# A two-layer decode kernel (cached attention and a gated feed-forward): one load of keys per layer cut by columns, its last columns brought in by five transfers of unequal height

## The chip, the cores and the metric

The kernel runs on one core of a Trainium2 chip. The metric is the device time of one execution in microseconds (us); lower is better. An engine here is one of the core's compute engines (TensorE = PE, VectorE = DVE, ScalarE = ACT, GpSimd = POOL) or the queue SP, which issues every transfer of this kernel. "DMA engine" means one of the sixteen movers that carry the transfers' rows.

## The reference, cut to what matters

Two layers, each an attention block over a cache followed by a feed-forward block, for 4 sequences of one token:

```python
def _A_ref(x, k_cache, v_cache, wq, wo):           # 32 query heads, 8 key heads, Dh = 128
    q = (x @ wq) as (4, 32, 1, 128)
    scores = einsum("bhqd,bhkd->bhqk", q, k) * Dh ** -0.5     # 8192 cached keys
    o = einsum("bhqk,bhkd->bhqd", softmax(scores), v)
    return o as (4, 1, 4096) @ wo
def _B_ref(x, w_gate, w_up, w_down):
    return (silu(x @ w_gate) * (x @ w_up)) @ w_down
...
for two layers:
    x = x + _A_ref(_layernorm(x), A_k_cache, A_v_cache, A_wq, A_wo)
    x = x + _B_ref(_layernorm(x), B_w_gate, B_w_up, B_w_down)
```

Both layers read the same caches and weights. Keys and values are 67 MB each in bf16 and are read almost wholly in each layer, so the work is mostly reading: 272.90 MB by the page.

## The kernel before, in words

**Units and slots.** The work of a layer is 16 units: a unit u is one sequence and one pair of key heads (`pair_gb`). Each unit has a load of keys, K(L, u), and one of values, V(L, u), of 4 MB each: 128 partitions with a row of 32 KB (16384 bf16 numbers) per partition, contiguous in memory. A load goes to one of four slots (five in layer 1) of the tile `kvf`; a slot is eight column blocks of 4 KB per partition (`NB = 8`, `BW` numbers wide), named `s{slot}.{q}`.

**What is done with a load.** For keys, `turn` (line 482) transposes each of the eight blocks on DVE in place, then `scores` (line 506) runs four matmuls on the block on PE; `max_p`, `exps` and `turn_p` make the probabilities. For values, `products` (line 608) runs the matmuls; DVE then gathers them (`gather`, lines 660 and 663).

**What sets the order of the loads.** The list `cmds`, written out before any instruction is emitted: K of unit 0, then K and V in turn, V one unit behind; the output weights `wo` in four parts in between; at a layer's end the weights of the feed-forward ("W", "W+"). An entry is (item, slot, first block, end block). `placed` gives slots in turn; some loads are given in halves or in smaller parts there. `pump` issues the next entries of the list as soon as all blocks of an entry are free; `freed` calls it whenever blocks are done with. All go through the queue of SP, in order: `load` calls `T.dma` (line 93), which puts the waits on SP, issues one transfer and counts its semaphore up by 16 on completion. A load of all eight blocks uses the slot's own semaphore (`sem_s`), a partial one a semaphore of its own (`part_sem`).

**Around the change.** `order[0][4]` is the fifth unit of layer 0, `order[1][5]` the sixth of layer 1. The fifth K of layer 0 goes to slot 3, after the third K, and is followed on SP by a V and by the last part of `wo`; the sixth K of layer 1 goes to slot 2, and is followed by a V.

**How the pieces are released.** Slot 3 held keys, which `finished` frees block by block as PE is through with each; slot 2 held values, which are freed by halves of four blocks.

Of the kernel before, what the change touches and what calls it, by code (L numbers as in the profile page):

```python
# [20 lines left out]
class _Sync:  # L21
# [69 lines left out]
    def dma(self, engname, out_ap, in_ap, sem, reads=(), writes=()):  # L91
        self._wait(engname, self._need(reads, writes))
        ins = self.eng[engname].dma_start(out_ap, in_ap)  # L93
        k = id(sem)
        self.semval[k] = self.semval.get(k, 0) + 16
        ins.then_inc(sem, 16)
        self._record(engname, (sem, self.semval[k]), reads, writes)
        return ins

    def wait_res(self, engname, reads=(), writes=()):  # L100
        self._wait(engname, self._need(reads, writes))


def bass_interleave_layers__gqa_block_cached__swiglu_ffn__decode_kernel(
# [18 lines left out]
    P = 128  # L123
# [6 lines left out]
    NB = 8  # L130
# [14 lines left out]
    with ExitStack() as es:  # L145
# [3 lines left out]
        BW = TB * Dh  # L149
# [6 lines left out]
        kv = kvf[:, 0:(NSLOT + 1) * SL].rearrange("p (s w) -> p s w", s=NSLOT + 1)  # L156
# [104 lines left out]
        sem = lambda name: es.enter_context(nc.semaphore(name))  # L261
# [9 lines left out]
        def part_sem():  # L271
# [4 lines left out]
        T = _Sync(engines, prog)  # L276
# [6 lines left out]
             reads=["ident"], writes=["ident"])  # L283
        T.op("pool", lambda e: e.memset(quad[:], 0.0), writes=["quad"])
        for a in range(NA):
# [10 lines left out]
             reads=["ident"], writes=["head"])  # L296
# [3 lines left out]
             reads=["ident"], writes=["made"])  # L300
        T.op("dve", lambda e: e.tensor_reduce(sel[:].rearrange("p (h r) -> p h r", h=2),
                                              made.rearrange("p (h q r) -> p h r q", h=2, q=QH), AX.X, ALU.max),
             reads=["made"], writes=["sel"])
        T.op("dve", lambda e: e.tensor_reduce(own[:], made.rearrange("p (h q r) -> p q h r", h=2, q=QH),
                                              AX.XY, ALU.max),
             reads=["made"], writes=["own"])
# [7 lines left out]
        def pair_gb(u):  # L314
            return u // B, u % B

        order = [list(range(NP)), [NP - 1, NP - 2, NP - 3] + list(range(NP - 3))]
        turn_of = {}

        K = lambda L, u: ("K", L, u)  # L320
# [13 lines left out]
        def placed(seq, ring, parts):  # L334
            out = []
            for i, it in enumerate(seq):
                s = ring[i % len(ring)]
                out += parts[i](it, s) if i in parts else [(it, s, 0, NB)]
            return out
# [4 lines left out]
        cmds = placed(seq, (0, 1, 2, 3), {len(seq) - 1: ends})  # L344
# [7 lines left out]
        s = W_SLOT[0]  # L352
# [5 lines left out]
        assert W_SLOT[1] == ring[len(seq) % len(ring)]  # L358
        cmds += [(("W", 1), W_SLOT[1], 0, NB), (("W+", 1), W_SLOT[1], NB, NB + 1)]

        free = {(s, q) for s in range(NSLOT) for q in range(NB)}
        slot_of = {}
        issued = [0]
# [36 lines left out]
        def pump():  # L400
            while issued[0] < len(cmds):
                it, s, a, b = cmds[issued[0]]
                if it[0] == "wo":
                    load_weight(*it)
                else:
                    need = {(s, q) for q in range(a, b)}
                    if not need <= free:
                        return
                    free.difference_update(need)
                    if it[0] in ("W", "W+"):  # L410
                        load_weight(it[0], it[1], s)
                    else:
                        slot_of[it] = s
                        load(it, a, b, sem_s[s] if b - a == NB else part_sem())
                issued[0] += 1
# [3 lines left out]
        def load(it, a, b, sm):  # L419
            kind, L, u = it  # L420
            s = slot_of[it]
            gp, bt = pair_gb(u)
            src = (A_k_cache if kind == "K" else A_v_cache)[bt, 2 * gp:2 * gp + 2, :, :].rearrange(
                "h (p t) d -> (h p) (t d)", t=TT)
            over = WQ if s == QS and not q_gone else []
            q_gone.update(over)
            T.dma("sp", kv[:, s, a * BW:b * BW], src[:, a * BW:b * BW], sm,
                  writes=[f"s{s}.{q}" for q in range(a, b)] + over)

        def freed(s, a, b):  # L430
            free.update((s, q) for q in range(a, b))
# [403 lines left out]
        for kt in range(KT):  # L835
            T.op("pe", lambda e: e.matmul(xb[:, kt * B:(kt + 1) * B], lhsT=xio[:, pick2(kt)],
                                          rhs=ident[0:B, 0:B], is_transpose=True, start=True, stop=True),
                 reads=["pb", "ident"], writes=[f"pb{OUTB}"], sig=(kt == KT - 1))
# [62 lines left out]
```

## Time and profile before

| | |
|---|---|
| median of 2 runs | 649.96 us (649.75 to 650.18) |
| the profiled execution | 649.47 us |
| its span, first to last instruction | 647.7 us |
| busy, share of the span | PE 66%, DVE 65%, ACT 6%, POOL 2% |
| bytes read by transfers | 272.90 MB |
| chain that ended last, by engine | DMA 61%, DVE 24%, PE 9% |
| SP issuing one load of keys | 327 ns at the least, 328 in the median |

The median is of unprofiled runs, so a sum that is made on the profiled execution (649.47) stands 0.49 below it. The span leaves out 1.8 us of the execution. In the views, "SPq" is SP's queue as it issues a transfer, "kvf<-in_A_k_cache_dram" is a load of keys into the slots, and "us to landing" runs from a transfer's issue to its sixteenth semaphore count. The queue "hardware_dynamic" carries the kernel's own transfers; "instruction" are packets that bring the engines' own instructions, on the same DMA engines.

### The profile page before, as it was taken

What the parts mean: (1) busy time and instruction counts of PE and PEld (TensorE: products, weight loads), DVE (VectorE), ACT (ScalarE), POOL (GpSimd) and SP (SyncE); (2) the same over time, 40 slices, a digit from 0 to 9 for tenths busy, and PEclk for the clock granted to TensorE, in tenths of its full rate; (3) what the DMA queues carried; (4) which work ended last, traced back from release to release, by engine and by line L of the source; (5) the groups of instructions that cost most, each with busy time, mean ns of one, the idle gap of its engine ahead of it and who ended that gap; (6) DMA issues with size and microseconds to landing.
All of it is one profiled execution on the core that took longest, in us unless ns stands there. A gap on an engine that the chain in (4) does not pass through costs nothing.

```text
span 647.7 us, 7963 instructions
## 1 busy us (share of the span) xinstructions
PE 429.5 (66%) x3356; PEld 185.2 (29%) x3356; DVE 422.7 (65%) x703; ACT 39.1 (6%) x109; POOL 11.1 (2%) x43
## 2 busy tenths in 40 slices
PE   2584467466776665767866988767656567666866
PEld 2221122122222222323236333223222222222235
DVE  1585467466776666777852878968766667766943
ACT  1000000000000000000010010000000000000010
POOL 0000000000000000000000000000000000000000
PEclk9996796688977789876975799997778898777976
DMA  9999999999999999999999999999999999999996
GB/s 365 442 423 419 445 426 423 424 439 430 425 435 435 422 438 433 422 442 424 426 413 405 402 433 436 431 428 435 430 431 431 428 431 434 429 428 436 428 413 246
DMA packets 14771, 273.41 MB, mean 422 GB/s; under 512 B 1416, under 2 KB 1424, under 8 KB 5648
## 3 DMA queue, kind: packets, MB, share of 16 engines
q1 hardware_dynamic: 14736, 272.91, 98.9%
q8 instruction: 26, 0.43, 0.3%
q14 instruction: 9, 0.07, 0.0%
HBM read 272.90 MB, written 0.00 MB: 421 GB/s over the span
## 4 chain that ended last, share of the span: by engine, by line
DMA 61%; DVE 24%; PE 9%; issue 3%; another core or an unknown queue 1%; SPq 1%; ACT 0%; DVEq 0%; ACTq 0%
DMA kvf<-in_A_k_cache_dram 51%; DVE kvf L482 18%; DMA kvf<-in_A_v_cache_dram 7%; PE ps L506 4%; DMA kvf<-in_B_w_down_dram 4%; DVE pT L547 2%; PE ps L608 2%; DVE pb L663 2%; SPq L93 1%; PE ps L742 1%; DVE pb L660 0%; DVE kvf L447 0%; PE ps L517 0%; PE ps L697 0%
## 5 line engine op out<-in xcount | busy, mean ns | idle before, releaser
L506 PE MATMUL ps<-kvf,zq 128*128 128x512 bf16 x1024 | 300.3, 434 | 166.9 <-DVE kvf L482 162.5
L482 DVE STREAM_TRANSPOSE kvf<-kvf 128x1024 f32<-128x1024 f32 x246 | 290.2, 1216 | 135.1 <-DMA kvf<-in_A_k_cache_dram 134.8
L506 PEld LDWEIGHTS ps<-kvf,zq 128*128 128x128 bf16 x1024 | 94.7, 108 | 322.1 <-DVE kvf L482 224.5
L608 PE MATMUL ps<-kvf,pT 128*32 128x512 bf16 x960 | 67.1, 402 | 9.2 <-DVE pT L547 9.2
L533 ACT ACTIVATE pb<-ps,tiny 128x512 bf16<-128x512 f32 x32 | 22.0, 687 | 549.9 <-DVE tiny L531 369.7
L547 DVE STREAM_TRANSPOSE pT<-pb 64x512 bf16<-64x512 bf16 x60 | 40.9, 682 | 1.0
L663 DVE SCALAR_TENSOR_TENSOR pb<-ps,tiny,pb 128x128 f32<-128x128 f32 x96 | 33.7, 351 | 5.4 <-PE ps L608 2.1
L608 PEld LDWEIGHTS ps<-kvf,pT 128*32 128x32 bf16 x960 | 21.9, 98 | 37.6 <-issue 22.6
L512 DVE TENSOR_REDUCE tiny<-ps 128x1 f32<-128x512 f32 x32 | 21.9, 685 | 5.1 <-PE ps L506 4.5
L668 PEld LDWEIGHTS ps<-sel,pb 128*128 128x128 f32 x64 | 16.7, 274 | 18.0 <-DVE pb L663 10.1
L520 DVE TENSOR_REDUCE m<-ps 1x8 f32<-1x128 f32 x32 | 8.8, 275 | 17.9 <-PE ps L517 17.9
L496 POOL TENSOR_TENSOR zq<-scr,tiny 128x64 bf16<-128x64 bf16 x30 | 9.0, 299 | 562.4 <-PE ps L506 562.4
L668 PE MATMUL ps<-sel,pb 128*128 128x8 f32 x64 | 12.9, 274 | 6.2 <-DVE pb L663 6.2
L551 PE MATMUL ps<-rsm,tiny 128*128 128x8 f32 x64 | 12.0, 261 | 6.3 <-ACT rsm L535 6.3
L551 PEld LDWEIGHTS ps<-rsm,tiny 128*128 128x128 f32 x64 | 10.6, 198 | 18.8 <-ACT rsm L535 16.2
L528 PEld LDWEIGHTS ps<-m,tiny 1*128 1x128 f32 x64 | 10.0, 194 | 15.9 <-issue 13.3
L528 PE MATMUL ps<-m,tiny 1*128 1x8 f32 x64 | 12.9, 272 | 0.8 <-DVE rl L554 0.3
L660 DVE TENSOR_SCALAR pb<-ps,tiny 128x128 f32<-128x128 f32 x32 | 10.1, 316 | 3.4 <-PE ps L608 3.4
L554 DVE RECIPROCAL rl<-ps 128x8 f32<-128x8 f32 x32 | 5.6, 176 | 7.8 <-PE ps L551 7.8
L697 PE MATMUL ps<-oT,wo_sb 128*128 128x4 bf16 x256 | 7.7, 165 | 4.1 <-DVE oT L688 4.1
L742 PE MATMUL ps<-xn,kvf 128*128 128x4 bf16 x256 | 7.6, 166 | 3.6 <-DMA kvf<-in_A_wq_dram 2.8
L535 ACT ACTIVATE rsm<-head,tiny 128x8 f32<-128x8 f32 x32 | 9.6, 300 | 1.0
(73 smaller groups left out, 119.2 us busy)
## 6 DMA issues: line engine op xcount, KB each, us to landing
kvf<-in_A_k_cache_dram SPq DMA_DIRECT2D x28, 4096.0 KB, 32.0
kvf<-in_A_v_cache_dram SPq DMA_DIRECT2D x27, 4096.0 KB, 36.4
kvf<-in_A_v_cache_dram SPq DMA_DIRECT2D x4, 2048.0 KB, 19.0
kvf<-in_A_k_cache_dram SPq DMA_DIRECT2D x4, 2048.0 KB, 9.5
kvf<-in_A_wq_dram SPq DMA_DIRECT2D x2, 2048.0 KB, 9.7
wo_sb<-in_A_wo_dram SPq DMA_DIRECT2D x4, 1024.0 KB, 41.7
kvf<-in_A_v_cache_dram SPq DMA_DIRECT2D x4, 1024.0 KB, 34.8
kvf<-in_B_w_gate_dram SPq DMA_DIRECT2D x2, 1792.0 KB, 25.4
```

The costliest lines, as they stand in the source:

```text
L482: T.op("dve", lambda e: e.transpose(w, w), reads=[f"s{s}.{q}"], writes=[f"s{s}.{q}"])
L506: T.op("pe", lambda e: e.matmul(bank(bk)[:, 0:SW], lhsT=zq[:, z0:z0 + P], rhs=w[:, :, c // 2, :, c % 2], start=(q == 0 and c == 0), stop=( ...
L512: T.op("dve", lambda e: e.tensor_reduce(mx[:], bank(bk)[:, 0:SW], AX.X, ALU.max), reads=[f"pb{bk}"], writes=["mx"])
L528: T.op("pe", lambda e: e.matmul(at, lhsT=onesf[0:1, :].to_broadcast([1, P]), rhs=m8[:, turn_of[u], :], start=True, stop=True), reads=[f"m8 ...
L533: T.op("act", lambda e: e.activation(pb[:], bank(bk)[:, 0:SW], ACTF.Exp, bias=nm, accum_out=rs), reads=[f"pb{bk}", "nm"], writes=PB + ["rs"])
L547: T.op("dve", lambda e: e.transpose(dst, pb[hp]), reads=["pb"], writes=[name])
L551: T.op("pe", lambda e: e.matmul(at, lhsT=ones, rhs=rsm[:], start=True, stop=True), reads=["rsm", "onesf"], writes=[name])
L608: T.op("pe", lambda e: e.matmul(bank(k)[j * QB:(j + 1) * QB, q0 * Dh:q1 * Dh], lhsT=p_t[:, t, h, :], rhs=v[:, q0:q1, t, :], start=(h == 0 ...
L660: T.op("dve", lambda e: e.tensor_scalar(acc, o, own[:, 0:1], None, op0=ALU.mult), reads=[f"pb{k}", "own"], writes=PB)
L663: T.op("dve", lambda e: e.scalar_tensor_tensor(acc, o, own[:, q:q + 1], acc, op0=ALU.mult, op1=ALU.add), reads=[f"pb{k}", "own", "pb"], wr ...
L668: T.op("pe", lambda e: e.matmul(at, lhsT=acc, rhs=sel[:], start=True, stop=True), reads=["pb", "sel"], writes=[name])
L742: T.op("pe", lambda e: e.matmul(at[:, h * B:(h + 1) * B], lhsT=wq_sb[:, kt, h * Dh:(h + 1) * Dh], rhs=xn[:, kt * B:(kt + 1) * B], start=(k ...
```

## The change

In `cmds`, the entry of K(0, order[0][4]) and that of K(1, order[1][5]) are replaced by two: blocks 0 to 6 (28 KB of each row), and block 7 (the last 4 KB of each row). The second entry is not one transfer of 128 partitions but five, of 112, 8, 4, 2 and 2 partitions, in this order, with one semaphore that counts to 80. Both entries get a semaphore of their own instead of the slot's. Every other load is issued as before, by a function that now takes a list of cuts, with one cut from 0 to 128.

```diff
+    def dma_rows(self, engname, out_ap, in_ap, sem, cuts, reads=(), writes=()):
+        self._wait(engname, self._need(reads, writes))
+        k = id(sem)
+        for a, b in zip(cuts[:-1], cuts[1:]):
+            self.eng[engname].dma_start(out_ap[a:b], in_ap[a:b]).then_inc(sem, 16)
+            self.semval[k] = self.semval.get(k, 0) + 16
+        self._record(engname, (sem, self.semval[k]), reads, writes)
...
+        uneven = set()
+        for it in (K(0, order[0][4]), K(1, order[1][5])):
+            i, c = next((i, c) for i, c in enumerate(cmds) if c[0] == it)
+            cmds[i:i + 1] = [(it, c[1], 0, NB - 1), (it, c[1], NB - 1, NB)]
+            uneven.add((it, 1))
...
-            T.dma("sp", kv[:, s, a * BW:b * BW], src[:, a * BW:b * BW], sm,
-                  writes=[f"s{s}.{q}" for q in range(a, b)] + over)
+            T.dma_rows("sp", kv[:, s, a * BW:b * BW], src[:, a * BW:b * BW], sm,
+                       (0, 112, 120, 124, 126, P) if (it, b - a) in uneven else (0, P),
+                       writes=[f"s{s}.{q}" for q in range(a, b)] + over)
```

On SP this is what the two places become, in the built program's order (numbers per partition, two bytes each):

```
layer 0                                         layer 1
K 128x14336   waits for PE and DVE              K 128x14336   waits for PE
K 112x2048    waits for PE and DVE              K 112x2048
K   8x2048                                      K   8x2048
K   4x2048                                      K   4x2048
K   2x2048  twice                               K   2x2048  twice
V 128x16384   waits for PE                      V 128x16384   waits for PE and DVE
```

PE, ACT and POOL keep their instructions in their order. On DVE the first and the eighth transpose of the two K wait for the two new semaphores, where the first waited for the slot's.

## The prediction

> **What bounds the kernel now.** I read the page from the transfers inwards, since parts 2 and 3 answer at once whether the DMA engines ever rest. First the busy share of the sixteen DMA engines over 40 slices, their rate, and the queues:
>
> ```profile
> DMA  9999999999999999999999999999999999999996
> GB/s 365 442 423 419 445 426 423 424 439 430 425 435 435 422 438 433 422 442 424 426 413 405 402 433 436 431 428 435 430 431 431 428 431 434 429 428 436 428 413 246
> ...
> q1 hardware_dynamic: 14736, 272.91, 98.9%
> q8 instruction: 26, 0.43, 0.3%
> q14 instruction: 9, 0.07, 0.0%
> ```
>
> The stream never stops before the last slice, and 98.9% of the sixteen engines' time is the kernel's own packets. The rate is flat near 430 GB/s but for the start, the layer boundary (slices 21 to 23, 402 to 413) and the end. PE and DVE at 66% and 65% have a third of their time left. The chain of waits names the places where the stream sets the time:
>
> ```profile
> 68.09 31.96 DMA kvf<-in_A_k_cache_dram
> ...
> 326.74 23.68 DMA kvf<-in_B_w_down_dram
> 350.47 1.06 PE ps L818 x32
> ...
> 589.43 44.74 DMA kvf<-in_A_v_cache_dram
> 634.22 0.62 PE ps L608 x16
> ```
>
> The columns are start, length, what. A load of keys issued at 68.09 lands 31.96 later, though a load takes about 9.7 alone (below): some 22 us of other transfers stand ahead of it. The last two links are the ones that bind: the feed-forward of layer 0 starts when its last weights have landed (350.42), and the tail of the kernel when the last piece of values has (634.17). Behind that stands 13.5 us of serial work to 647.7. So only what brings those two landings forward or back counts.
>
> SP's queue shows the two places of the change, layer 0 and layer 1:
>
> ```profile
> 68.09 0.33 SPq L93 DMA_DIRECT2D kvf<-in_A_k_cache_dram  x1
> 70.70 0.33 SPq L93 DMA_DIRECT2D kvf<-in_A_v_cache_dram  x1
> 71.08 0.43 SPq L93 DMA_DIRECT2D wo_sb<-in_A_wo_dram  x1
> ...
> 391.74 0.33 SPq L93 DMA_DIRECT2D kvf<-in_A_k_cache_dram  x1
> 402.99 0.33 SPq L93 DMA_DIRECT2D kvf<-in_A_v_cache_dram  x1
> ```
>
> After the K, SP has 2.61 us free in layer 0 and 11.25 in layer 1.
>
> Last, not on the page, the trace's semaphore counts and packets one by one. Every transfer on 128 partitions adds sixteen, one per DMA engine. The first load of keys counts from 22.26 to 24.38, a spread of 2.1 us; the last piece of values from 629.55 to 634.18, a spread of 4.6. So the DMA engines do not keep step, and the landing is that of the slowest. Followed packet by packet (an engine's next packet starts within 20 ns of the last one's end), what sets an engine back is the "instruction" queues: each 16 KB packet of q8 costs its engine some 1.55 us, its own 1.0 to 1.1 and a slowed neighbour, and each 8 KB packet of q14 0.7 to 1.0. In layer 0 the q8 packets go round eight engines in turn. The four engines that carried the four rows of x at the start (four packets of 1 KB, one on each) are never among them; they and four others get only q14, one of the four three times. At the end eight engines stand 2.3 to 4.7 us behind the first, and the worst of the rest 3.9.
>
> **The change part by part.** *Prices of rows*, from landings. The V issued at 70.70 landed 39.1 later, at 109.80; the K before it at 68.09 + 32.0 = 100.09; so a load of eight 32 KB rows per engine is 9.71, 1.214 a row. A `wo` part issued at 35.09 landed 33.3 later, at 68.39, behind a V that landed at 34.72 + 31.1 = 65.82: 2.57 for sixteen 4 KB rows per engine, 0.161 a row. On a line through both, a row costs 0.011 and 0.0376 per KB, so a 28 KB row is 1.064.
>
> *Splitting by columns.* Each engine's eight rows become eight of 28 KB and, evenly dealt, eight of 4 KB: 8.51 + 1.29 = 9.80 against 9.71, 0.09 more per layer for each engine. All of it is on the stream.
>
> *Uneven dealing.* Of the 4 KB rows, the x rows show that a narrow transfer puts one row on each of as many engines, always engines outside the q8 round. I take it that 112 partitions give seven rows to each of sixteen engines, 8 give one to each of the eight engines outside the round, and 4, 2 and 2 fall to the first of these. Then the round's eight get 7 rows, four get 8, two get 9, two get 11. Per layer: the round's eight 8.51 + 7 x 0.161 = 9.64, that is 0.07 less than 9.71; the next four 0.09 more; two 0.25 more; two 8.51 + 1.77 = 10.28, 0.57 more. A transfer's closing semaphore packet is 9 ns; one to five more per engine are under 0.05 and within the rounding.
>
> *What of it reaches the end.* In layer 0 the last landing is that of one of the round's eight (two stand some 3.2 back at the last weights), so 350.42 comes 0.07 earlier and with it layer 1's loads, which wait for PE there. In layer 1 the worst of the round's eight again carries the landing at 634.17: 0.07 more. Sum -0.14, from 0 if the row price is a little higher to -0.30 if the second cut costs nothing (4 KB at 0.152 taken away twice). Above, if the two engines with 11 rows were the last ones, 2 x 0.57 = +1.14. I take -0.14: the eight hold the last place in both layers.
>
> *SP.* The K's issue of 0.33 becomes six of 0.33, 1.98, and one wait more. In layer 0 the first piece may go when block 6 is through, before 68.09, and five remain: 1.65 of the 2.61 before the V's own wait ends. In layer 1 all six fit in 11.25. Queued behind are V and `wo`, then K; nobody is late. Without that cover the V would be issued 1.65 later, into a backlog of 22 us, and cost nothing still; from that backlog on it would cost one for one.
>
> *Waits on DVE.* The first transpose now waits for 28 KB rows alone and may start 1.2 earlier; the eighth waits for the five pieces. Between them stand seven transposes of 1.14 to 1.2 each (8 us), so a landing 0.57 later is hidden. If it were not, PE's scores and the slot's release would be late by at most that, again into the backlog. An earlier start is worth nothing either, as the next load is already queued.
>
> [...]
>
> **The rivals.** *The overloaded two end last.* One engine outside the round has three q14 packets in layer 1 and stands 0.8 short of the last. With 11 rows twice it gains 0.57 + 0.07 on the round's eight in each layer and may pass them in layer 0, where it is within 0.7 of the last. For: nothing shows which of the four engines it is. Against: two of four are loaded so. Price: at most +1.14, as above, so up to 651.1; with one layer +0.3.
>
> *The 112 rows are not spread over sixteen engines.* Slower: no row of this trace has a height that is not a multiple of 16, but for x with 4. On n engines each takes 112 / n rows of 0.161, against seven. On one engine 18.0, 16.9 more than its seven, per layer: since every later load needs that engine too, both reach the end, 650 + 34 = 684. On two, 9.0, 7.9 more: 666. On four, 3.4 more: 657. It decides (2%, 13 us) from two engines down. The x rows on four engines speak against it.
>
> [...]
>
> *A transfer's fixed time stays in the queue.* The nearest row of a transfer alone is the store of the output, 4 KB: 0.29 to issue and 1.0 that SP waits for it, 1.3. If each of the ten more held the stream for that, +13: 663. Against it stands the `wo` part, with at most 0.14: ten times that is 651.4. [...]
>
> *The split frees the slot's waiters earlier and this shows.* Faster: 1.2 us earlier on DVE, twice, 647.6; from slots to landing there are 22 us of backlog, so no.
>
> That the change is not made at all is out: SP's program has the ten pieces.
>
> **How the numbers follow.** Forecast, the round's eight carry the end: 0.72. The overloaded two: 0.20. Rows of 112 on few engines, 0.03, fixed times 0.01. Earlier release 0.01. Something that no row shows, 0.03. The profiled execution has 649.47 - 0.14 = 649.33; the median of the runs shown stands 0.49 above it, and I give the time in its terms: 649.96 - 0.14 = 649.8. The range goes from 649.8 less the spread of the runs (0.7) and the other 0.16 of the gain, 648.9, to 650.18 plus 1.14, 651.3. Two per cent is 13 us, about what a measurement of this kernel can tell from no change: only the 112 rows on one or two engines, the fixed times and half of the unknown pass it. Faster 0.01, within 0.95, slower 0.04.
>
> **What would show it.** In the changed kernel's trace: four or five narrow issues of 0.33 on SP behind the K at 68 and at 392; the V behind at 70.7 and 403 as before; the landing of the last piece of values 0 to 0.3 earlier, its sixteen counts closer together; packets of 4 KB 256 more. Wrong would be: a gap in the stream near 100 or 419, one engine tens of rows behind, a spread at the end over 4.6, or a last landing later than 634.2.

## The result, and the profile after

The changed kernel takes 654.47 us (median of 2 runs, 654.02 to 654.92) against 649.96: a ratio of 1.0074, 95% interval 1.0058 to 1.0091. That is within the 2% and yet clearly slower, by 4.5 us; the prediction had 649.8, and its range ended at 651.3. The profiled span went from 647.7 to 653.1.

The page of the changed kernel, DMA share, rate and queues:

```profile
DMA  9999999999999999999999999999999999999996
GB/s 376 428 423 420 438 406 391 422 435 426 439 425 431 434 422 442 423 437 424 433 407 404 392 436 434 377 426 431 432 425 429 434 429 434 427 434 432 430 410 234
...
q1 hardware_dynamic: 15056, 272.91, 98.8%
q8 instruction: 26, 0.43, 0.3%
q14 instruction: 9, 0.07, 0.0%
```

The bytes are the same and the engines look as busy as before, in every slice. But the rate has two dents that were not there: 406 and 391 in the sixth and seventh slice (82 to 114 us; 426 and 423 before), and 377 in the 26th (408 to 425; 431 before). These are the two places of the change. "Busy" here is the time that a packet took, however slowly it went.

SP's queue in the changed kernel, at the two places (L104 is the `dma_start` in the new `dma_rows`):

```profile
66.96 2.81 SPq L104 DMA_DIRECT2D kvf<-in_A_k_cache_dram  x6
70.75 0.35 SPq L104 DMA_DIRECT2D kvf<-in_A_v_cache_dram  x1
...
394.30 2.10 SPq L104 DMA_DIRECT2D kvf<-in_A_k_cache_dram  x6
405.55 0.35 SPq L104 DMA_DIRECT2D kvf<-in_A_v_cache_dram  x1
```

Nothing is late there: the V is issued at 70.75 (70.70 before), and in layer 1 at 405.55, which is 402.99 plus the 2.56 that layer 0 had lost by then. The chain of waits shows what came of it:

```profile
66.96 33.53 DMA kvf<-in_A_k_cache_dram
...
329.69 23.30 DMA kvf<-in_B_w_down_dram
353.03 1.05 PE ps L833 x32
...
594.54 44.45 DMA kvf<-in_A_v_cache_dram
639.03 1.04 PE ps L623 x16
```

The last weights of layer 0 land at 352.99 instead of 350.42, 2.57 later; the last piece of values at 638.99 instead of 634.17, 4.82 later. Each place costs 2.2 to 2.6 us, and together they hold 4.8 of the 5.4 that the span grew by. The V behind the changed K of layer 0 landed 41.3 after its issue at 70.75, at 112.05, against 109.80: 2.25 of the loss is there within some ten microseconds of the change.

To see it, one cuts out 96 to 102 us, in which the 4 KB rows pass. In these windows the columns are the stretch, its length, busy time of PE, PEld, DVE, ACT and POOL, the granted clock, the DMA share, and GB/s. First the kernel before, then the changed one:

```profile
96.00:102.00 6.00, 0.63 (x2) 0.28 (x3) 1.93 (x2) 0.00 (x0) 0.00 (x0) 0.56 1.00 431
102.00:112.00 10.00, 9.98 (x37) 4.09 (x35) 9.83 (x17) 1.08 (x3) 0.00 (x0) 0.75 1.02 419
```

```profile
96.00:102.00 6.00, 0.19 (x1) 0.13 (x2) 1.49 (x2) 0.00 (x0) 0.00 (x0) 0.50 1.03 274
102.00:112.00 10.00, 9.65 (x37) 3.90 (x36) 9.86 (x17) 1.08 (x3) 0.00 (x0) 0.81 0.95 397
```

The DMA share is 1.03, full, and the rate 274 for 431: 36% of six microseconds is 2.2 us. In the trace's packets of that stretch a 4 KB row takes 284 ns in the median (96.5 to 98 us), not the 160 of the sum, and the 28 and 32 KB rows that other engines are moving at that time take up to 2.17 and 2.13 us instead of 1.07 and 1.22. So the rows of the new transfers are slow, and what is beside them at that time is slow too.

The place in layer 1 shows the same, before and after:

```profile
414.00:424.00 10.00, 7.50 (x56) 2.53 (x54) 8.98 (x15) 0.00 (x0) 0.30 (x1) 1.00 1.04 447
```

```profile
414.00:424.00 10.00, 8.45 (x60) 2.80 (x59) 9.10 (x15) 1.08 (x3) 0.30 (x1) 1.00 1.03 346
```

447 GB/s became 346, and that is 2.3 us of the ten.

### The profile page after: what moved, and what is told of

It reads as the page before. It is cut to its first block, busy times and chain, and to the rows that moved or that the text cites. A ratio compares the mean times of both kernels' runs of the same rounds, so it can differ in the third digit from the quotient of the medians.

```text
span 653.1 us, 7974 instructions
## 1 busy us (share of the span) xinstructions
PE 429.6 (66%) x3356; PEld 185.3 (28%) x3356; DVE 422.6 (65%) x703; ACT 39.1 (6%) x109; POOL 11.1 (2%) x43
## 4 chain that ended last, share of the span: by engine, by line
DMA 61%; DVE 26%; PE 6%; issue 4%; another core or an unknown queue 1%; SPq 1%; ACT 0%; DVEq 0%; ACTq 0%
DMA kvf<-in_A_k_cache_dram 51%; DVE kvf L497 19%; DMA kvf<-in_A_v_cache_dram 7%; DMA kvf<-in_B_w_down_dram 4%; PE ps L623 2%; DVE pT L562 2%; DVE pb L678 2%; PE ps L521 1%; SPq L93 1%; PE ps L757 1%; DVE pb L675 0%; DVE kvf L462 0%; PE ps L532 0%; PE ps L712 0%
## 5 line engine op out<-in xcount | busy, mean ns | idle before, releaser
L543 PEld LDWEIGHTS ps<-m,tiny 1*128 1x128 f32 x64 | 10.1, 197 | 15.2 <-issue 12.8
L675 DVE TENSOR_SCALAR pb<-ps,tiny 128x128 f32<-128x128 f32 x32 | 10.1, 317 | 3.4 <-PE ps L623 3.4
```

The lines of the kernel that those rows point to most:

```text
L543: T.op("pe", lambda e: e.matmul(at, lhsT=onesf[0:1, :].to_broadcast([1, P]), rhs=m8[:, turn_of[u], :], start=True, stop=True), reads=[f"m8 ...
L675: T.op("dve", lambda e: e.tensor_scalar(acc, o, own[:, 0:1], None, op0=ALU.mult), reads=[f"pb{k}", "own"], writes=PB)
```

## The experiments

Three theories went in. *Height*: a transfer that is not 128 high deals the partitions to the DMA engines otherwise, and engines then meet at the same partitions. *Columns*: 4 KB rows 32 KB apart in memory are slow. *Narrow*: transfers of 8, 4, 2 and 2 partitions hold up the engines. Edits are shown against the changed kernel; each time stands beside runs of the kernel before on the same chip.

**e1_cols_only**

```diff
-                       (0, 112, 120, 124, 126, P) if (it, b - a) in uneven else (0, P),
+                       (0, P),
```

> The two K are cut by columns as in the change (28 KB and 4 KB of each row), but the 4 KB come as one transfer of 128 partitions. Three theories for the 2.2 us per layer that the change lost. Height: a transfer of 112 partitions deals the partitions to the sixteen DMA engines otherwise than one of 128, engines meet on the same partitions and slow each other and the loads beside them. Columns: 4 KB rows that stand 32 KB apart in memory are read slowly at any height. Narrow: the transfers of 8, 4, 2 and 2 partitions hold up the engines. Height and narrow say 650.1 here (0.09 per layer for shorter rows), with 4 KB packets of 0.16 us; columns says 654.4, with 4 KB packets near 0.3 us.

Measured 649.59 against 649.10, ratio 1.0004 (0.9995 to 1.0013). The window:

```profile
96.00:102.00 6.00, 1.85 (x5) 0.71 (x6) 3.08 (x5) 0.00 (x0) 0.00 (x0) 0.58 1.02 434
```

434 GB/s: the dent is gone, and the 4 KB rows there take 159 ns in the median and 172 at the most. Columns falls. The split by itself costs nothing that can be told from zero.

**e2_112_16**

```diff
-                       (0, 112, 120, 124, 126, P) if (it, b - a) in uneven else (0, P),
+                       (0, 112, P) if (it, b - a) in uneven else (0, P),
```

> As the change, but block 7 comes as two transfers of 112 and 16 partitions, none narrower than sixteen, so that each DMA engine gets eight rows of 4 KB. Height says the loss stays, 653.5 to 654.5, and 4 KB packets near 0.3 us from the first rows on; narrow says 650.1; columns says 654.4. With even dealing the spread of the landings should not grow in any theory.

Measured 653.50 against 649.10, 1.0068 (1.0055 to 1.0081), nearly all of the loss:

```profile
96.00:102.00 6.00, 0.23 (x1) 0.13 (x2) 1.54 (x2) 0.00 (x0) 0.00 (x0) 0.50 1.01 264
```

Narrow transfers are not needed for it, nor is uneven dealing: here each engine has eight rows, if the 112 are dealt seven to each of sixteen. Narrow falls as the main cause.

**e3_64_64**

```diff
-                       (0, 112, 120, 124, 126, P) if (it, b - a) in uneven else (0, P),
+                       (0, 64, P) if (it, b - a) in uneven else (0, P),
```

> As the change, but block 7 comes as two transfers of 64 partitions, four rows of 4 KB for each engine in each. Height says that engines meet in pairs if each takes four neighbouring partitions, so that a 4 KB row takes up to twice 0.16: 8 x 0.16 = 1.3 us more per layer, 652.6, and less than that if the dealing keeps the engines apart; narrow says 650.1; columns says 654.4.

Measured 654.54 against 649.10, 1.0084 (1.0069 to 1.0099):

```profile
96.00:102.00 6.00, 0.00 (x0) 0.00 (x0) 1.04 (x1) 0.00 (x0) 0.00 (x0) 0.63 1.06 263
```

Two tall, even transfers of 64 rows lose no less than the change. Height had the direction and missed the size: +5.4, where meeting in pairs was to give +2.6.

**e4_narrow_alone**: the K of both layers uncut, and in layer 0

```diff
+                    T.dma_rows("sp", wres[112:, 0:BW], src[112:, (NB - 1) * BW:], part_sem(), (0, 8, 12, 14, 16),
+                               writes=["wu0"])
```

> The kernel before, but behind the fifth K of layer 0 stand four more transfers of 8, 4, 2 and 2 partitions with 4 KB rows, a second copy of the last rows of that K, which go to columns that nothing uses yet; layer 1 is as before. Narrow says that about all of the loss of one layer comes: 652.1. Height says that at most the extra rows show, 0.16 to 0.6 us on the eight engines that carry them, which are not the last ones: 650.0 to 650.3. Columns says the same as height, as few rows are involved.

Measured 650.32 against 649.10, 1.0016 (1.0007 to 1.0025): +1.0 to +1.2, between the theories.

```profile
96.00:102.00 6.00, 0.00 (x0) 0.00 (x0) 0.73 (x1) 0.00 (x0) 0.00 (x0) 0.59 0.99 377
```

32 KB rows beside the narrow ones took up to 1.88 us. So sixteen narrow rows do some of it too, more than the 0.16 to 0.6 us that they add to the engines which carry them, and less than one layer's 2.2.

What is it about height: which partitions an engine writes, or which rows of memory it reads? The next four bring the two K as eight transfers of sixteen whole 32 KB rows. Each engine has eight rows, one of each transfer, if sixteen rows are dealt as the rows of the change were (8, 4, 2 and 2 rows gave as many semaphore counts, 112 gave sixteen); only which ones go together differs. A pair of names says where the sixteen rows are written and from where they are read: "near" is sixteen neighbours (`slice(16 * j, 16 * j + 16)`), "far" every eighth (`slice(j, P, 8)`), for j from 0 to 7.

```diff
-        for a, b in zip(cuts[:-1], cuts[1:]):
-            self.eng[engname].dma_start(out_ap[a:b], in_ap[a:b]).then_inc(sem, 16)
+        for o, i in cuts:
+            self.eng[engname].dma_start(out_ap[o], in_ap[i]).then_inc(sem, 16)
```

**e5_near_near** and **e6_far_far**

> The same two K come with whole 32 KB rows, uncut by columns, as eight transfers of sixteen partitions: sixteen neighbours each, rows of memory likewise. Each DMA engine has one row per transfer and eight in all, as before. Two theories of where engines meet. [...] Read side: what matters is which rows of memory are read at once. This kernel alone tells only that height matters: by either theory 690 to 710, if height alone costs as much as with 64 partitions (twice), 669.

> As e5_near_near, but each of the eight transfers takes every eighth partition, and every eighth row of memory. [...] Read side: some other time than near too, but for the memory's sake; the two crossed kernels tell.

**e7_near_far** and **e8_far_near**

> Eight transfers of sixteen rows again, written to sixteen neighbouring partitions but read from every eighth row of memory. The keys come to other partitions than they should, so the two units' scores go with other rows; nothing is left out. Write side: the time of e5_near_near, about 700. Read side: the time of e6_far_far, about 669.

> Eight transfers of sixteen rows, written to every eighth partition and read from sixteen neighbouring rows of memory; again the keys of two units come to other partitions. Write side: the time of e6_far_far, about 669. Read side: the time of e5_near_near, about 700.

| written to | read from | us (before 648.93) | packet of 32 KB in the K, median |
|---|---|---|---|
| 16 neighbours | 16 neighbours | 690.79 and 701.16 | 3.5 to 4.0 us |
| 16 neighbours | every eighth | 688.29 and 697.81, 1.068 (1.0506 to 1.0854) | 4.2 us |
| every eighth | every eighth | 673.19 and 673.23, 1.0374 (1.0344 to 1.0404) | 2.4 to 2.6 us |
| every eighth | 16 neighbours | 673.16 and 677.95, 1.0410 (1.0323 to 1.0498) | 2.3 to 2.6 us |

The two runs of each kernel written to neighbours differ by some 10 us, so the first two rows are not told apart, nor are the last two; but the slowest run of the last two rows is 10 us faster than the fastest of the first two. The windows, first of the kernel before, then in the order of the table, one kernel in each fence:

```profile
92.00:108.00 16.00, 7.22 (x32) 2.87 (x25) 7.79 (x13) 0.40 (x1) 0.00 (x0) 0.68 0.97 415
```

```profile
92.00:108.00 16.00, 0.54 (x12) 0.04 (x4) 0.00 (x0) 0.00 (x0) 0.00 (x0) 0.68 0.94 128
```

```profile
92.00:108.00 16.00, 0.65 (x12) 0.11 (x4) 0.00 (x0) 0.00 (x0) 0.00 (x0) 0.59 1.01 124
```

```profile
92.00:108.00 16.00, 0.82 (x16) 0.21 (x8) 0.16 (x1) 0.00 (x0) 0.00 (x0) 0.67 1.03 217
```

```profile
92.00:108.00 16.00, 0.63 (x12) 0.11 (x4) 0.00 (x0) 0.00 (x0) 0.00 (x0) 0.58 0.98 207
```

What is written decides: 128 and 124 GB/s to sixteen neighbours, 217 and 207 to every eighth partition, whatever is read; 415 in this stretch before. The read side falls. The write side had the order right and the sizes roughly: about 700 and 669 were the author's estimates, against 688 to 701 to neighbours and 673 to 678 to every eighth. What it is in the writing that engines meet at, and how many of them at a time, is not shown; what is shown is that a packet of 32 KB took 3.5 to 4.2 us to neighbours and 2.3 to 2.6 to every eighth, where one takes 1.21 to 1.22 in the median of the kernel before.

**e9_extra_own** and **e10_extra_other**: is it enough that an engine keeps to the partitions that it has in a transfer of 128? Theory Own says so. For it the author took partitions 0 to 31, every fourth in each transfer, as the engines' own, and 64 to 95 as those of others; the trace does not name a row's partition, so that choice is an assumption. The kernel before, with four extra transfers of 8 partitions in layer 0, base 0 or 64:

```diff
+                    T.dma_rows("sp", wres[:, 0:BW], src[:, (NB - 1) * BW:], part_sem(),
+                               [slice(base + j, base + 32, 4) for j in range(4)], writes=["wu0"])
```

> The kernel before with four extra transfers of 8 partitions, 4 KB rows, behind the fifth K of layer 0: a second copy of rows of that K, to columns that nothing uses yet. [...] Own: no packet beside them slows; four rows of 0.16 more on eight engines, which are not the last ones but for one: 0 to +0.5 us, 649 to 649.6, and 32 KB packets near 100 us stay at 1.22. Rival, narrow transfers are dear whatever partitions they write to: twice the +1.0 that sixteen such rows cost in e4, 651.

> [...] Own: the rows meet those engines' rows, the 32 KB packets near 100 us rise to about 1.5 to 1.9, and the time goes up by about twice the +1.0 of e4: 651. Rival, narrow transfers are dear whatever partitions they write to: the same time as e9_extra_own. Both kernels alike and near 649.3 would say that e4's cost came from something else, as its two-high transfers.

Measured 649.78 for own, 1.0005 (0.9996 to 1.0014), and 651.07 for other, 1.0025 (1.0016 to 1.0035), beside 649.42. First partitions 0 to 31, then 64 to 95:

```profile
96.00:102.00 6.00, 0.81 (x2) 0.27 (x3) 2.12 (x2) 0.00 (x0) 0.00 (x0) 0.50 1.00 426
```

```profile
96.00:102.00 6.00, 0.00 (x0) 0.00 (x0) 0.54 (x1) 0.00 (x0) 0.00 (x0) 0.50 0.99 339
```

The two kernels issue the same number of transfers, of the same height and size; only the partitions differ, and with them the rows of memory that are read, which the four crossed kernels have ruled out. With 0 to 31 the narrow rows take 159 ns and the 32 KB rows beside them 1.21 to 1.23 us, as if nothing were there; with 64 to 95 285 ns (98 to 99.5 us) and some 1.84 us, at most 1.92. So a transfer 8 high costs nothing measurable as such; which partitions it writes is what costs. That the dear ones are being written by another engine of the full stream is the author's explanation: the pair came out as Own said, in its order and in its packets, but which engine writes which partition is not shown. Transfers 4 and 2 high were not tried on partitions 0 to 31.

**e11_two_blocks**

```diff
-            cmds[i:i + 1] = [(it, c[1], 0, NB - 1), (it, c[1], NB - 1, NB)]
-            uneven.add((it, 1))
+            cmds[i:i + 1] = [(it, c[1], 0, NB - 2), (it, c[1], NB - 2, NB)]
+            uneven.add((it, 2))
```

> As the change, but the uneven transfers carry blocks 6 and 7, 8 KB of each row, instead of 4 KB. If the loss goes with the bytes that engines write to partitions of others, it doubles: +9 us, 658. If it is a cost per transfer (ten more of them, as in the change), it stays: +4.5, 653.5.

Measured 659.48 against 649.42, 1.0149 (1.0130 to 1.0168): +10.1, or 2.2 times the change's 4.5. With the number of transfers unchanged, twice the bytes lose about twice as much. Between other shapes the loss is not in proportion to the bytes: 32 rows cost 1.65 us in e10, and the 128 of one layer 2.2 to 2.6 in the change.

## Why the prediction was wrong, point by point

- *What bounds the kernel*: right. The two landings that were named moved, by 2.57 and 4.82, and the end with them: the span grew by 5.4, of which 0.6 came behind the last landing. Of the prediction's own signs of being wrong one came, a last landing later than 634.2; no gap shows in the stream, which went on at a lower rate.
- *How the rows are dealt*: right as to how many engines. That 112 rows go to sixteen, seven to each, was the author's assumption, with no run behind it then. The five transfers left 36 separate semaphore counts: 16 + 8 + 4 + 2 + 2 as rows landed, and one more for each of the four narrow ones at its issue (69.0 to 70.0 us). How many rows each engine took, and which engines took the narrow ones, the counts do not say.
- *The price of a row*: the step that failed. "The round's eight 8.51 + 7 x 0.161 = 9.64, that is 0.07 less" took 0.161 from a transfer of 128 partitions. In the transfers of 112 and less, as the author concludes from e2, e3 and the pair of e9 and e10, engines write partitions that others are writing; the trace does not name a row's partition, so this is not shown. A row cost 0.28, and, what the sum had no term for at all, the 28 and 32 KB rows beside it cost up to 1.1 and 0.9 more. Instead of -0.07 each layer lost 2.2 to 2.6. The price in its own place (128 high, e1) was 0.16 as reckoned.
- *The split by columns*: right, 0.09 per layer reckoned, +0.5 us in two layers measured with an interval of -0.3 to +0.8.
- *SP, and the waits on DVE*: right in that neither costs anything; the V of layer 0 was issued at 70.75. The first transpose of layer 0 did not start 1.2 us earlier, as it might have: with the 28 KB rows slowed as well, it started at 100.51 instead of 100.07.
- *A transfer's fixed time*: rightly held to be small. The 0.14 that stood against +13 us is the 2.57 of the `wo` part, 1 MB, less a quarter of the 9.71 of a load of 4 MB; e9 has four more transfers at +0.4, not different from none, and e11 twice the loss with no transfer more.
- *The rival of 112 rows on few engines*: it pointed at the right transfer for the wrong reason. They were on sixteen engines, by their sixteen counts.
- *The rival of the two overloaded engines*: not seen. The spread of the last piece's sixteen counts went from 4.6 to 3.9, as dealing the work unevenly was to do, but with even dealing it is 3.75 in e1 and 4.0 in e2, so this is not shown to be the change's doing.
- *The chances*: "something that no row shows" had 0.03. It was a surprise only to a sum that let a row of one shape stand for another. The only narrow load of the kernel before, x with four rows of 1 KB, took 46 ns a row and slowed nothing that shows, but with 4 KB in all it could not bound the price of 512 KB. So 0.161 was one end of that price, not the middle.

What stays open is the size. If the rows of two halves of 64 went at half of the 430 GB/s, they would lose about 1.2 us per layer (64 rows of 4 KB at half the rate, twice; an estimate), and they lost 2.7. Engines stand up to 2 us apart (the sixteen counts of the K before ran from 98.12 to 100.04), so rows of the transfers before and behind may be met too; whether that is the difference was not tried. No version was found that beats the kernel before. To relieve an engine that lags, another must, by theory Own, write to that engine's partitions, and if e10's rows are such, they are dear: 1.65 us for 32; whether some smaller number of them would still gain was not tried.

## What to carry to other kernels

In a full stream like this one (some 430 GB/s), keep loads 128 partitions high and cut them by columns, which cost nothing measurable here (e1, 1.0004), not by partitions (e2 and e3, 1.0068 and 1.0084); the change's cut by partitions slowed the transfers beside it as well, 32 KB rows from 1.22 us to as much as 2.13, so look at their packets too. A DMA share of 1.0 says that engines are occupied, not that they move bytes (1.03 at 274 GB/s here, 1.00 at 431 before): read the GB/s of the stretch beside it. When a price is taken from a row of another shape, give the missing shape a bound of its own: 0.16 us for 4 KB became 0.28.

## What the runs showed of the hardware that was not expected

Transfers that write to sixteen neighbouring partitions moved 124 to 128 GB/s, and those to every eighth partition 207 to 217, whichever of the two sets of memory rows was read (e5 to e8, 92 to 108 us); transfers of 128 moved some 430 (before, 16 to 100 us). Thirty-two rows of 4 KB, 128 KB in all, cost 1.65 us of a 649 us kernel when they went to partitions 64 to 95 (0.3 us at 430 GB/s), and nothing measurable when they went to partitions 0 to 31 (e10 and e9).
